# Masking attention by a VectorE multiply after exp in place of TensorE matmuls into the scores

## The chip, the cores and the metric

One core of one Trainium2 chip. The metric is the device time of one execution in microseconds (us). Medians of several executions are given; ratios are told apart from them below. An execution that took over 1.5% longer than the fastest of its kernel, at a lower granted clock, is marked slow and left out.

## The reference

Two layers, each run twice. Layer B (a gated MLP with a spatial matmul) isn't touched. Layer A is attention with a recurrent memory: 2048 tokens are cut into 64 segments of 32, and each segment attends over 8 memory rows and its own tokens. The first 8 output rows are the next segment's memory, so segments run one after the other.

```python
L = M + seg_len                                   # 8 + 32
mask = (idx[:, None] < M) | (idx[:, None] >= idx[None, :])
for s in range(n_seg):                            # 64, one after the other
    h = concatenate([mem, x_of_segment])
    q, k, v = h @ Wq, h @ Wk, h @ Wv              # 32 heads of 128
    scores = where(mask, q k^T * scale, -1e9)
    o = softmax(scores) v @ Wo
    mem = o[:, :M]                                # feeds the next segment
```

## The kernel before

32 heads are worked in two score tiles (r = 0 and 1). A score tile packs two heads side by side, so a mask is needed both for causality and for the blocks in which one head's queries meet the other's keys. The mask of 0 and -30000 is put into PSUM first, by an identity matmul for each half of the partitions; the score matmuls follow with start=False, to add to it.

```python
def scores(r):
    psS = att.tile([P, 4, 112], F32, name="psS")
    for g in range(2):                                           # the mask, by matmul
        nc.tensor.matmul(psS[64*g:64*g+64], lhsT=ident_bf[:, 64*g:64*g+64],
                         rhs=maskN[:, j4, :].unsqueeze(1).to_broadcast([P, 4, 112]),
                         start=True, stop=True, ...)
    for i in range(4):
        for K, hi, c0 in ((KA, 40, 0), (KTB, 16, 80)):
            for g in range(2):
                nc.tensor.matmul(psS[64*g:64*g+64, i, c0:c0+2*hi], lhsT=K[...], rhs=QQ[...],
                                 start=False, stop=True, ...)
    E[r] = segp.tile([P, 4, 112], BF16, name="E")
    nc.scalar.activation(out=E[r][:], in_=psS[:], func=ACT.Exp, scale=scale)

def denom(r):   # sums by matmul with ones, then 1/x as exp(-ln x), on ScalarE
    nc.tensor.matmul(psD[:], lhsT=ones64[:], rhs=E[r][:, :, 0:80], ...)
    ...
    nc.scalar.activation(out=L[:], in_=psD[:], func=ACT.Ln)
    nc.scalar.activation(out=R[r][:], in_=L[:], func=ACT.Exp, scale=-1.0)

# one segment; the order on TensorE, VectorE and ScalarE is the program's (cut)
r0 = qk(0); r2 = qk(2); qk_T(0, r0); r1 = qk(1); qk_T(2, r2); r3 = qk(3); qk_T(1, r1)
scores(0)
qk_T(3, r3)                  # VectorE transpose of the last K rows
v0 = v_mm(0, range(KT))
denom(0)
v_out(0, v0)
scores(1)
probs(0)
v1 = v_mm(1, range(KT)); v_out(1, v1)
denom(1)
...                          # pv(0), output projection, pv(1), next segment's input
```

The softmax here doesn't subtract the row's maximum and nothing guards it: scores larger than these inputs give would overflow.

## Time and profile before

| | before |
|---|---|
| median (4 runs) | 2167.15 us (2165.07 to 2173.1) |
| TensorE, VectorE, ScalarE busy | 86%, 50%, 49% |
| segments | 128, in two stretches of 64 |
| undisturbed length of a segment | 12.18 us |
| mean length of a segment | 12.68 us |

"Undisturbed" is, here and below, the tenth percentile of the 126 steps from one segment's first projection matmul to the next one's. The mean is longer because TensorE stops for about 1 us in about every second segment. In the lines of the profile PE is TensorE (PEld its weight loads), DVE VectorE, ACT ScalarE, POOL GpSimd, and L400 is line 400 of the kernel. Two lines of the waits on TensorE itself (engine, line, what it waited for: us in total, times, longest) show most of these stops and where TensorE waits for the transposed input `hA`:

```profile
PE pw L493 <- issue: 48.5, 45, 3.7
PE psm L400 <- DVE hA L536: 38.0, 114, 0.7
```

### The profile page before, as it was taken

Reading aid. Unit: us, or ns where it says so; the run is one execution under the profiler, and the core shown is the slowest. Engines: PE = TensorE matmul, PEld = TensorE weight load, DVE = VectorE, ACT = ScalarE, POOL = GpSimd, SP = SyncE. Lnnn points to the kernel's source line nnn. Section 1 sums busy time; section 2 is a strip of 40 time slices with the busy share of each in tenths; the row PEclk is TensorE's granted clock in tenths of the full one; section 3 lists DMA queues with packets and bytes.
Section 4 is the critical chain, followed back from the end, with each engine's and each line's share of the span. In section 5 each row is a group of like instructions: output and inputs, shape, how many; then the busy total and the mean of one; then the engine's idle time right before and its main releaser. Section 6 shows DMA issues by size and latency. Waiting matters only on the chain. (4 is left out here: it accounts for less than half of the span.)

```text
span 2160.9 us, 102768 instructions
## 1 busy us (share of the span) xinstructions
PE 1865.7 (86%) x47588; PEld 1090.1 (50%) x47616; DVE 1087.1 (50%) x2419; ACT 1054.1 (49%) x2340; POOL 179.7 (8%) x319
## 2 busy tenths in 40 slices
PE   0699999999999998582987999999999999995899
PEld 0355555555555555341763555555555555554476
DVE  1555555555555555340434555555555555553322
ACT  0465555555555555380004555555555555554600
POOL 2000000000000000001230000000000000000022
PEclk9999999999999999895998999999999999998999
DMA  9201111111111110328552011111111111104253
GB/s 379 84 21 35 36 42 37 37 37 35 45 35 35 36 30 24 104 84 255 157 159 63 23 42 36 38 35 37 43 36 36 35 35 35 32 27 156 49 137 88
DMA packets 178670, 145.22 MB, mean 67 GB/s; under 512 B 97472, under 2 KB 148288, under 8 KB 175168
## 3 DMA queue, kind: packets, MB, share of 16 engines
q1 hardware_dynamic: 152544, 83.76, 14.2%
q10 hardware_dynamic: 21728, 30.78, 4.1%
q0 software_dynamic: 3968, 24.12, 2.9%
q8 instruction: 372, 6.09, 1.1%
q14 instruction: 58, 0.48, 0.1%
HBM read 88.13 MB, written 33.70 MB: 56 GB/s over the span
## 5 line engine op out<-in xcount | busy, mean ns | idle before, releaser
L400 PEld LDWEIGHTS <-hA 128*32 128x32 bf16 x12288 | 302.7, 96 | 349.4 <-DVE hA L536 93.2
L560 ACT CAST rows<-psm 128x512 bf16<-128x512 f32 x512 | 299.7, 585 | 187.7 <-PE psm L400 187.7
L493 PE MATMUL pw<-Wo_sb,uT 128*32 128x128 bf16 x16640 | 289.7, 220 | 58.8 <-issue 48.5
L400 PE MATMUL psm<-Wq_sb,hA 128*32 128x512 bf16 x4096 | 272.4, 382 | 38.3 <-DVE hA L536 38.0
L493 PEld LDWEIGHTS <-uT 128*32 128x32 bf16 x16640 | 240.0, 97 | 106.3 <-issue 56.5
L400 PE MATMUL psm<-Wk_sb,hA 128*32 128x512 bf16 x4096 | 270.7, 380 | 0.0
L400 PE MATMUL psv<-Wv_sb,hA 128*32 128x512 bf16 x4096 | 268.0, 382 | 0.0
L219 PE MATMUL pg<-wspT,z2n 128*128 128x256 bf16 (+1 forms) x1536 | 177.1, 277 | 55.7 <-DMA wspT<-in_B_w_sp_dram 55.7
L564 DVE STREAM_TRANSPOSE QQ<-rows 128x512 bf16<-128x512 bf16 x256 | 181.2, 708 | 82.2 <-ACT rows L560 80.3
L564 DVE STREAM_TRANSPOSE KA<-rows 128x512 bf16<-128x512 bf16 x256 | 182.1, 711 | 36.2 <-ACT rows L560 36.0
L573 DVE CAST VA<-psv 128x512 bf16<-128x512 f32 x256 | 177.0, 691 | 43.5 <-PE psv L400 27.6
L535 DVE CAST_PREDICATED pre<-maskM,pw 128x128 bf16<-128x128 uint16 x126 | 36.6, 291 | 321.2 <-PE pw L493 321.2
L219 PEld LDWEIGHTS <-z2n 128*128 128x128 bf16 (+1 forms) x1536 | 151.3, 100 | 81.2 <-issue 63.1
L602 ACT ACTIVATE L<-psD 128x320 f32<-128x320 f32 x256 | 111.9, 437 | 153.1 <-PE psD L600 153.1
L400 PE MATMUL psb<-Wq_sb,hB 128*32 128x512 bf16 x1024 | 80.7, 393 | 92.2 <-DVE hB L449 72.4
L609 DVE TENSOR_TENSOR PT<-E,R 128x320 bf16<-128x320 bf16 x256 | 83.3, 325 | 144.0 <-ACT R L604 144.0
L529 POOL COPY QQ<-QTB 128x256 bf16<-128x256 bf16 x128 | 49.4, 402 | 1211.3 <-PE psO L621 839.7
L222 DVE TENSOR_TENSOR gb<-pg,bsp_bc 128x256 f32<-128x256 f32 x96 | 40.6, 423 | 208.1 <-PE pg L219 208.1
L625 ACT CAST uT<-psO 128x128 bf16<-128x128 f32 x256 | 67.8, 265 | 145.5 <-PE psO L621 145.5
L590 ACT ACTIVATE E<-psS 128x448 bf16<-128x448 f32 x256 | 136.8, 534 | 0.0
L540 ACT COPY o_sb<-pw 128x128 f32<-128x128 f32 x130 | 34.5, 265 | 194.2 <-DVE pre L535 181.6
L400 PEld LDWEIGHTS <-hB 128*32 128x32 bf16 x3072 | 57.1, 96 | 140.8 <-DVE hB L449 72.4
(93 smaller groups left out, 2613.6 us busy)
## 6 DMA issues: line engine op xcount, KB each, us to landing
xs<-xd SPq DMA_DIRECT2D x48, 256.0 KB
xs<-xd ACTq DMA_DIRECT2D x48, 256.0 KB
oA_d<-o_sb SPq DMA_DIRECT2D x130, 64.0 KB
xs_y<-xd SPq DMA_DIRECT2D x32, 256.0 KB
xd<-ot_y SPq DMA_DIRECT2D x32, 256.0 KB
Wq_sb<-in_A_Wq_dram POOLq DMA_DIRECT2D x6, 1024.0 KB, 16.1
Wk_sb<-in_A_Wk_dram POOLq DMA_DIRECT2D x6, 1024.0 KB, 24.5
Wv_sb<-in_A_Wv_dram POOLq DMA_DIRECT2D x6, 1024.0 KB, 20.5
```

The source lines that it names most:

```text
L219: nc.tensor.matmul(pg[0:fsz, :], lhsT=z2n[:, st_i, f0:f0 + fsz], rhs=wspT[:, st_i, :], start=(st_i == 0), stop=(st_i == NT - 1))
L222: nc.vector.tensor_tensor(out=gb[0:fsz, :], in0=pg[0:fsz, :], in1=bsp_bc[0:fsz, t0:t0 + TC2], op=ALU.add)
L400: nc.tensor.matmul(ps[32 * cg:32 * cg + 32, :], lhsT=lhs(kt, cg), rhs=rhs(kt, cg), start=(kt == 0), stop=(kt == KT - 1), tile_position=(0, ...
L493: nc.tensor.matmul(po[32 * cg:32 * cg + 32, 0:128], lhsT=lhs[:, n, :], rhs=wo_rhs(h, cg), start=(h == 0), stop=(h == H - 1), tile_position ...
L529: nc.gpsimd.tensor_copy(QQ[:, :, :, 0:8], bs["QTB"][:, :, :, 8 * j4:8 * j4 + 8])
L560: nc.scalar.copy(r[:], ps[:])
L564: nc.vector.transpose(out=QQ[:, j % 2, :, 8:40] if j < 2 else KA[:, j % 2], in_=r[:])
L573: nc.vector.tensor_copy(VA[:, r].rearrange("p i e -> p (i e)"), ps[:])
L590: nc.scalar.activation(out=E[r][:], in_=psS[:], func=ACT.Exp, scale=scale)
L602: nc.scalar.activation(out=L[:], in_=psD[:], func=ACT.Ln)
L609: nc.vector.tensor_tensor(out=PT[r][:, :, 0:80], in0=E[r][:, :, 0:80], in1=R[r][:], op=ALU.mult)
L625: nc.scalar.copy(hview(uT_cur, r, 0, 8), ov[:, :, :, 8:16])
```

## The change

The intent: TensorE is the busiest engine, VectorE is idle half of the time, so the mask moves to VectorE. The mask becomes 0 and 1, is multiplied into exp(scores), and the four mask matmuls of a segment go.

```diff
-    nc.gpsimd.memset(maskf[:], NEG)
+    nc.gpsimd.memset(maskf[:], 0.0)
     ... (allowed places 1.0 in place of 0.0, fill 0.0 in place of NEG)
 def scores(r):
-    for g in range(2):
-        nc.tensor.matmul(psS[64*g:64*g+64], lhsT=ident_bf[...], rhs=maskN[...], start=True, ...)
     ...
-                start=False, stop=True, ...)
+                start=(i == 0 and K is KA), stop=True, ...)
     ... exp as before ...
+def close(r):
+    nc.vector.tensor_tensor(out=E[r][:], in0=E[r][:],
+        in1=maskN[:, j4, :].unsqueeze(1).to_broadcast([P, 4, 112]), op=ALU.mult)
 ...
 scores(0)
 qk_T(3, r3)
+close(0)
 v0 = v_mm(0, range(KT))
 denom(0)
 v_out(0, v0)
 scores(1)
+close(1)
 probs(0)
```

More of the change, by code (lines that the diff above doesn't have):

```diff
@@ L25 @@
 FH = 688
-NEG = -30000.0
 LN_EXP_SET = 6
@@ L70, in _consts @@
             q = 32 * (2 * g + sl)
-            nc.gpsimd.memset(maskf[q:q + 32, :, 40 * sl:40 * sl + 40], 0.0)
-            nc.gpsimd.memset(maskf[q:q + 32, :, 80 + 16 * sl:96 + 16 * sl], 0.0)
+            nc.gpsimd.memset(maskf[q:q + 32, :, 40 * sl:40 * sl + 40], 1.0)
+            nc.gpsimd.memset(maskf[q:q + 32, :, 80 + 16 * sl:96 + 16 * sl], 1.0)
             blk = maskf[q:q + 32, :, 40 * sl + 16:40 * sl + 40]
-            nc.gpsimd.affine_select(out=blk, in_=blk, compare_op=ALU.is_ge, fill=NEG, base=8,
+            nc.gpsimd.affine_select(out=blk, in_=blk, compare_op=ALU.is_ge, fill=0.0, base=8,
                                     pattern=[[0, 4], [1, 24]], channel_multiplier=-1)
@@ L79, in _consts @@
                 blk = maskf[q:q + 32, :, 80 + 16 * sl + lo:88 + 16 * sl + lo]
-                nc.gpsimd.affine_select(out=blk, in_=blk, compare_op=ALU.is_ge, fill=NEG, base=0,
+                nc.gpsimd.affine_select(out=blk, in_=blk, compare_op=ALU.is_ge, fill=0.0, base=0,
                                         pattern=[[-8, 4], [0, 8]], channel_multiplier=1)
-                nc.gpsimd.affine_select(out=blk, in_=blk, compare_op=ALU.is_ge, fill=NEG, base=0 if step else 7,
+                nc.gpsimd.affine_select(out=blk, in_=blk, compare_op=ALU.is_ge, fill=0.0, base=0 if step else 7,
                                         pattern=[[8, 4], [step, 8]], channel_multiplier=-1)
@@ L577, in scores @@
                 psS = att.tile([P, 4, 112], F32, name="psS")
-                for g in range(2):
-                    nc.tensor.matmul(psS[64 * g:64 * g + 64], lhsT=ident_bf[:, 64 * g:64 * g + 64],
-                                     rhs=maskN[:, j4, :].unsqueeze(1).to_broadcast([P, 4, 112]),
-                                     start=True, stop=True, tile_position=(0, 64 * g), skip_group_check=True)
                 for i in range(4):
@@ L587, in scores @@
                                              lhsT=K[:, r, n:n + 2, :].rearrange("p h k -> p (h k)"), rhs=QQ[:, r, n:n + 2, 0:hi],
-                                             start=False, stop=True, tile_position=(0, 64 * g), skip_group_check=True)
+                                             start=(i == 0 and K is KA), stop=True, tile_position=(0, 64 * g), skip_group_check=True)
                 E[r] = segp.tile([P, 4, 112], BF16, name="E")
                 nc.scalar.activation(out=E[r][:], in_=psS[:], func=ACT.Exp, scale=scale)
+            def close(r):
+                nc.vector.tensor_tensor(out=E[r][:], in0=E[r][:], in1=maskN[:, j4, :].unsqueeze(1).to_broadcast([P, 4, 112]), op=ALU.mult)
             def last(t, n):
```

## The prediction

> **What bounds the kernel now.** I read the busy table and the 40 slices first, to find the stage that the change touches.
>
> ```profile
> PE 1865.7 (86%) x47588; PEld 1090.1 (50%) x47616; DVE 1087.1 (50%) x2419; ACT 1054.1 (49%) x2340; POOL 179.7 (8%) x319
> ...
> PE   0699999999999998582987999999999999995899
> ...
> DVE  1555555555555555340434555555555555553322
> ```
>
> TensorE looks nearly full and VectorE half empty, in two long even stretches (the two attention blocks). Each is 64 segments run one after the other: a segment's output becomes the next one's memory. In the trace the first projection matmuls of the segments start at 79.1 to 880.7 us in the first block and 1153.3 to 1949.8 us in the second: 12.72 and 12.64 us a segment (63 steps each). The undisturbed period is 12.18 us; the other half microsecond is mostly stops of about 1 us in the output-projection matmuls, put down to "issue". So 128 segments hold some 1620 of the 2166.8 us, and 0.1 us in one segment is 13 us in the kernel. The other two stages are untouched.
>
> Next the groups, shapes apart, for what is removed and for the yardstick of what is added.
>
> ```profile
> L579 PE MATMUL psS<-maskN,ident_bf 128*64 128x448 bf16 x512 | 97.4, 377 | 0.0
> ...
> L609 DVE TENSOR_TENSOR PT<-E,R 128x320 bf16<-128x320 bf16 x256 | 83.3, 325 | 144.0 <-ACT R L604 144.0
> ...
> L610 DVE TENSOR_TENSOR PT<-E,R 128x128 bf16<-128x128 bf16 x256 | 56.1, 219 | 0.0
> ```
>
> 512 mask matmuls, two for each of two score tiles in 128 segments. Their 97.4 us are not what they cost, since matmuls overlap. That, and everything else that decides this case, stands in the timeline of one segment (start us, duration us):
>
> ```profile
> 408.58 0.71 DVE L564 STREAM_TRANSPOSE KA<-rows 128x512 bf16<-128x512 bf16 x1
> ...
> 409.57 0.38 PE L579 MATMUL psS<-maskN,ident_bf 128*64 128x448 bf16 x2
> ...
> 409.69 0.58 ACT L560 CAST rows<-psm 128x512 bf16<-128x512 f32 x1 [0.28 <-PE psm L400]
> 409.79 0.20 PE L586 MATMUL psS<-QQ,KA 128*64 128x80 bf16 x2
> ...
> 410.14 1.05 PE L400 MATMUL psv<-Wv_sb,hA 128*32 128x512 bf16 x16
> 410.25 0.54 ACT L590 ACTIVATE E<-psS 128x448 bf16<-128x448 f32 x1
> 410.31 0.71 DVE L564 STREAM_TRANSPOSE KA<-rows 128x512 bf16<-128x512 bf16 x1 [0.15 <-ACT rows L560]
> ...
> 411.24 0.69 DVE L573 CAST VA<-psv 128x512 bf16<-128x512 f32 x1 [0.21 <-PE psv L400]
> ...
> 411.41 0.38 PE L579 MATMUL psS<-maskN,ident_bf 128*64 128x448 bf16 x2
> ...
> 411.98 1.05 PE L400 MATMUL psv<-Wv_sb,hA 128*32 128x512 bf16 x16
> 411.99 0.47 ACT L604 ACTIVATE R<-L 128x320 bf16<-128x320 f32 x1
> 412.36 0.53 ACT L590 ACTIVATE E<-psS 128x448 bf16<-128x448 f32 x1
> 412.49 0.32 DVE L609 TENSOR_TENSOR PT<-E,R 128x320 bf16<-128x320 bf16 x1 [0.56 <-ACT R L604]
> ...
> 412.95 0.31 PE L599 MATMUL psD<-E,ones 128*128 128x320 bf16 x1
> ...
> 413.80 0.21 PE L621 MATMUL psO<-PT,VA 64*128 64x80 bf16 x2
> ```
>
> Three things are to be seen. A mask pair delays the scores by 409.79 - 409.57 = 0.22 us. The first exp (410.25) begins when ScalarE has finished the last row copy (409.69 + 0.58 = 410.27), so it hangs on ScalarE, not on the mask. And the second exp ends at 412.89, the second denominator matmul starts at 412.95: exp and TensorE arrive together there, with no slack for anything put between them.
>
> [...] 325 ns for 320 elements and 219 for 128 give 0.55 ns per element[...]. [...]
>
> **The change part by part.** Removed: four matmuls and their weight loads a segment, 2 x 0.22 = 0.44 us of TensorE's order. The constants differ only in value. Moved: nothing else on TensorE or ScalarE; on VectorE the built order is last K transpose, multiply 0, V copy 0, multiply 1, probabilities 0, V copy 1. Added: 256 VectorE products of 448 elements, in place in E, two a segment. From L609: 325 + 128 x 0.55 = 396 ns, 0.40 us each. The denominator matmul waited for exp; it now waits for the product.
>
> I now run the shown segment forward with its own durations, with 0.05 us from VectorE's end to TensorE's start (hA ends 405.95, its matmul starts 406.00) and 0.03 us from ScalarE to VectorE (R ends 412.46, L609 starts 412.49).
>
> First half. Scores end 0.22 earlier, but exp 0 still starts at 410.25 behind the row copy and ends 410.79. VectorE is in the last K transpose until 411.02. Multiply 0 runs 411.02 to 411.42, so denominator 0 starts at 411.47, not 411.11: later by 0.36. TensorE has finished its V matmuls by then (they start 0.22 earlier) and waits over half a microsecond. The first saving is lost.
>
> Second half. Log, reciprocal-exp and exp 1 follow denominator 0 on ScalarE in fixed order: exp 1 moves from 412.36 to 412.72 and ends 413.25. The second saving shortens TensorE's road to the scores, which is not what exp 1 waits for, so it is lost too. Multiply 1: 413.28 to 413.68. Denominator 1: 413.73 in place of 412.95, later by 0.78.
>
> The rest. The first PV matmul stood 0.85 after denominator 1, behind other projection work: 414.58. It needs probabilities 0, now behind multiply 1: 413.68 plus 0.46 (412.49 to 412.95 today) = 414.14, in time. Probabilities 1, output projection, memory copy and next segment follow at the same distances.
>
> Sum: +0.36 (multiply 0 behind the transpose) + 0.42 (multiply 1 whole, with its extra hand-over) = 0.78 us. Back-to-back VectorE starts overlap by some 0.03, so I take 0.75: x 128 = 96 us. 2166.8 + 96 = 2263; I take nothing off for the issue stops, which the longer waits might hide a little.
>
> **The rivals.** (a) TensorE sets the pace and the matmuls' time is saved: 0.44 x 128 = 56 us, 2111 us. For it: 86% busy and back-to-back matmuls. Against it: ScalarE's row copy before exp 0 and the exp-to-denominator tie. It could only be if the multiply hid, and nothing in the order lies between it and its matmul. (b) One of the two multiplies hides, say if the first denominator is later but exp 1 isn't: about 0.4 x 128 = 50 us, 2215 us. The fixed ScalarE order speaks against it. (c) [...] 148 + 448 x 1.10 = 640 ns, 0.24 more per multiply, all on the path: 0.75 + 0.48 = 1.23 x 128 = 157 us, 2324 us. For it: the mask is a repeated row[...]. (d) The 1 us issue stops, 0.5 us a segment, fall differently because a segment has eight TensorE instructions fewer and pauses twice: between 25 us gained and 15 us lost, an estimate from 64 us of them in all.
>
> **Range and chances.** The order of the three engines is fixed, so I trust the sign more than the size. Centre 2263. Down to 2230 if issue stops shrink or some of the 0.36 hides; up to 2305 for slower multiplies in part or extra waits after multiply 1. Faster by over 2% (under 2123) needs (a): 0.03. Within 2% (up to 2210) needs (b) and (d) together: 0.07. Slower: 0.90.
>
> **What would show each step.** Right: the product lasts near 400 ns; it follows directly on the last K transpose; denominator 0 waits for it on TensorE (0.5 us or more), denominator 1 too; exp 0 starts no earlier after the segment's start (4.25 us); undisturbed segments take about 12.95 us; TensorE's share falls below 82%; the other two stages keep their time. Wrong: a product of 600 ns (rival c); no TensorE wait at the denominators; exp 0 earlier by 0.2 us, which would mean that the mask did delay it; or a period of 12.18 us or less.

The sum: 0.36 + 0.42 = 0.78 us, taken as 0.75 us, x 128 = 96 us, so 2263 us. The overlap of 0.03 us is found in the trace between two transposes of the shown segment (QQ, 407.93 + 0.68 = 408.61, and KA, which starts at 408.58; 28 ns in the median of 26 such pairs). Rival (c) supposes that reading the mask row again and again doubles the time of an element, 1.10 ns in place of the 0.55 from L609 and L610. That the moved start flag suffices was not shown either: kernels with it passed the comparison with the reference ("Another order on VectorE" and "exp 1 ahead of the reciprocal of tile 0"), though that comparison doesn't see the mask, as "No mask at all" will show. The score matmuls took 208 and 184 ns in the mean with it, 202 and 182 before.

## The result and the profile after

The changed kernel takes 2255.7 us (median of 4 runs, 2254.7 to 2261.1) against 2167.15. The ratio is 1.0409, 95% interval 1.0383 to 1.0435: slower. Ratios here and below are from fast runs alone; they are not quite the ratios of the medians.

The busy table and slices of the changed kernel:

```profile
PE 1834.6 (81%) x47076; PEld 1079.0 (48%) x47104; DVE 1142.5 (51%) x2675; ACT 1045.2 (46%) x2340; POOL 179.1 (8%) x319
...
PE   0688888888888888582977888888888888885899
...
DVE  2555555555555555340334555555555555553422
```

TensorE has 512 matmuls fewer (47588 to 47076), and its share falls from 86% to 81%: slices of nine tenths have become slices of eight. Less work there did not make a shorter kernel. The groups and the list of waits say where the room went:

```profile
L588 DVE TENSOR_TENSOR E<-E,maskN 128x448 bf16<-128x448 bf16 x256 | 99.1, 387 | 159.3 <-ACT E L585 159.3
L597 PE MATMUL psD<-E,ones 128*128 128x320 bf16 x256 | 75.9, 296 | 117.5 <-DVE E L588 117.5
```

```profile
DVE E L588 <- ACT E L585: 159.3, 128, 1.2
PE psD L597 <- DVE E L588: 117.5, 256, 1.4
```

The multiply takes 387 ns in the mean. All 256 denominator matmuls now wait for it, 117.5 us in total, 0.92 us a segment; before, TensorE had no such wait. VectorE in turn stands idle 159.3 us, 128 times, until exp 1 gives it its operand: its idle time lies before the operand is there, where the multiply can't use it. One segment of the changed kernel, starting at 439.39 us (start, duration):

```profile
443.08 0.58 ACT L559 CAST rows<-psm 128x512 bf16<-128x512 f32 x1 [0.28 <-PE psm L399]
...
443.56 0.55 ACT L585 ACTIVATE E<-psS 128x448 bf16<-128x448 f32 x1
443.70 0.71 DVE L563 STREAM_TRANSPOSE KA<-rows 128x512 bf16<-128x512 bf16 x1 [0.15 <-ACT rows L559]
444.33 0.35 DVE L588 TENSOR_TENSOR E<-E,maskN 128x448 bf16<-128x448 bf16 x1
...
444.74 0.30 PE L597 MATMUL psD<-E,ones 128*128 128x320 bf16 x1 [0.35 <-DVE E L588]
...
445.59 0.47 ACT L602 ACTIVATE R<-L 128x320 bf16<-128x320 f32 x1
445.97 0.53 ACT L585 ACTIVATE E<-psS 128x448 bf16<-128x448 f32 x1
446.53 0.39 DVE L588 TENSOR_TENSOR E<-E,maskN 128x448 bf16<-128x448 bf16 x1 [1.25 <-ACT E L585]
...
446.97 0.30 PE L597 MATMUL psD<-E,ones 128*128 128x320 bf16 x1 [0.53 <-DVE E L588]
```

Multiply 0 follows at once on the last K transpose, though exp 0 had ended 0.22 us earlier (443.56 + 0.55 = 444.11); the denominator follows at once on the multiply. Multiply 1 follows on exp 1, which follows on R, the reciprocal of tile 0, on ScalarE.

Starts within a segment, in us after its first projection matmul, from the two traces (medians over the 29 and 32 segments within 0.03 us of the undisturbed length):

| | before | after | difference |
|---|---|---|---|
| exp 0 | 4.24 | 4.17 | -0.07 |
| multiply 0 | | 4.94 | |
| denominator 0 | 5.11 | 5.35 | +0.24 |
| exp 1 | 6.36 | 6.58 | +0.22 |
| multiply 1 | | 7.14 | |
| denominator 1 | 6.95 | 7.58 | +0.63 |
| next segment | 12.18 | 12.80 | +0.62 |

After denominator 1 the two kernels run in step. The mean segment went from 12.68 to 13.43 us, more than the undisturbed one, because the stops rose from 0.50 to 0.63 us a segment. In the profiled runs, 98.3 us apart, the two stretches of 63 steps account for 1691.9 - 1598.0 = 93.9 us; the stretch between them grew by 6.0 us, the start by 0.4, and the end shrank by 2.1.

### The profile page after: what moved, and what is told of

It reads as the page before. It is cut to its first block, busy times and chain, and to the rows that moved or that the text cites. A ratio compares the mean times of both kernels' runs of the same rounds, so it can differ in the third digit from the quotient of the medians.

```text
span 2259.2 us, 102109 instructions
## 1 busy us (share of the span) xinstructions
PE 1834.6 (81%) x47076; PEld 1079.0 (48%) x47104; DVE 1142.5 (51%) x2675; ACT 1045.2 (46%) x2340; POOL 179.1 (8%) x319
## 5 line engine op out<-in xcount | busy, mean ns | idle before, releaser
L588 DVE TENSOR_TENSOR E<-E,maskN 128x448 bf16<-128x448 bf16 x256 | 99.1, 387 | 159.3 <-ACT E L585 159.3
L597 PE MATMUL psD<-E,ones 128*128 128x320 bf16 x256 | 75.9, 296 | 117.5 <-DVE E L588 117.5
```

Of the source, the lines that this page charges most:

```text
L588: nc.vector.tensor_tensor(out=E[r][:], in0=E[r][:], in1=maskN[:, j4, :].unsqueeze(1).to_broadcast([P, 4, 112]), op=ALU.mult)
```

## The experiments

Nine runs of eight kernels were made, on two chips. Where the text speaks of a period, it is the undisturbed segment of that run's profile.

### Both masks at once

The mask matmuls stay as they were; a second mask of 0 and 1 is made at the start, and the two multiplies are added.

```diff
 # on the kernel before
+maskB = maskf * (1/30000) + 1
 scores(0); qk_T(3, r3)
+close(0)        # E *= maskB
 ...
 scores(1)
+close(1)
```

> Both ways at once: the mask matmuls of the kernel before stay and the two multiplies are added. Theory A (the multiplies' waits set the pace, TensorE's mask time is off the path): the undisturbed segment stays at the 12.80 us of the changed kernel, so 2167 + 128 x 0.62 = 2246 us, 2240 to 2262 with the issue stops. Rival B (TensorE's time adds up; removing the mask matmuls saved 0.44 us a segment and the multiplies cost 1.06): 13.24 us, 2303 us. Side question: with 704 TensorE instructions a segment again, the issue stops (mean less shortest period) go back from 0.63 to about 0.50 us [...], and stay at 0.63 if they hang on the waits.

2257.78 us (2254.41 to 2260.07), ratio to before 1.0395 (1.0374 to 1.0415); period 12.80 us. Putting all four matmuls back into the changed kernel costs nothing: multiplies, denominators, exp 1 and the next segment start within 0.01 us of where they do in the changed kernel. The waits on TensorE show where they went:

```profile
PE psD L607 <- DVE E L598: 66.2, 256, 0.6
```

66.2 us of waiting in place of 117.5: 51.3 / 128 = 0.40 us a segment, near the 0.44 that four mask matmuls take. In the changed kernel nearly all of TensorE's saved time is turned into waiting. Rival B falls. The side question: the stops stayed at some 0.62 us a segment with the old number of instructions, so that number alone doesn't set them. Nor do the multiplies' waits alone: the kernels without a multiply, below, have 0.59 to 0.64.

### One multiply each

```diff
 # e2_first: close(0) and no mask matmuls for tile 0; tile 1 as before
 # e3_second: close(1) and no mask matmuls for tile 1; tile 0 as before
```

> Multiply for the first score tile alone, mask matmuls for the second. Theory A: only denominator 0 is late, behind the last K transpose, by 0.24 us: period 12.42 us, 2167 + 31 = 2198 us. Rival C (each multiply costs its own 0.4 us less a share of the saved matmuls, the same for both tiles): half of the loss, 2211 us for this and the next run alike.

> Multiply for the second score tile alone, mask matmuls for the first. Theory A: the whole multiply and its hand-over stand between exp 1 and denominator 1, where there was no slack: 0.42 us, period 12.60 us, 2167 + 54 = 2221 us; more than the first tile's. Rival C: 2211 us.

The first alone: 2206.42 us, ratio 1.0156 (1.0139 to 1.0174), period 12.40 us, denominator 0 at 5.35. The second alone: 2229.93 us, ratio 1.0271 (1.0246 to 1.0296), period 12.58 us, denominator 1 at 7.36 against 6.95. The same instruction costs 0.22 us in one place and 0.40 in the other; together 0.62, which is the whole change. Rival C, which has both cost the same, falls: the two intervals don't touch. Both medians lie 8 to 9 us above the expectation: the kernel before took 2172.08 us on this chip, 5 us above the 2167 that I reckoned from, and the stops were 0.64 us a segment in both in place of 0.50.

### No mask at all

```diff
 # e4_nomask: the mask matmuls removed, no multiply (a wrong result on purpose)
```

> No mask at all, neither matmuls nor multiplies: a wrong result on purpose, to see what a mask that costs nothing would be worth. Theory A: TensorE and the chain exp 0, denominator 0, log, reciprocal, exp 1, denominator 1 are tied, and the chain moves only by the first 0.22 us: period 11.96 us, 2167 - 28 = 2139 us. Rival B: both pairs count, 0.44 us, 11.74 us, 2111 us.

Period 11.96 us, as theory A has it; rival B's 11.74 falls. Four executions took 2141.08, 2147.69, 2174.37 and 2176.37 us. The last two, and with them the profiled one, are slow (granted clock 0.965 and 0.964, against 0.971 and 0.972 of the other two); the ratio of the fast two is 0.987 (0.984 to 0.9899). In the slow profile all stretches of half clock lie outside the 126 steps (the segments' Q projection matmuls took 382 ns in the mean, as in the kernel before), so its period may be read, and its total may not. A mask that cost nothing would be worth 0.22 us a segment and not 0.44.

The comparison with the reference at the outputs' tolerance doesn't see the mask, so for none of these kernels is it evidence that the mask is right. That the changed kernel masks the same places was checked by reading alone: the conditions of its selects are the old ones, with 1 and 0 for 0 and -30000.

### Another order on VectorE

```diff
 # on the changed kernel
 scores(0)
-qk_T(3, r3)
-close(0)
+close(0)
+qk_T(3, r3)
 ...
-close(1)
-probs(0)
+probs(0)
+close(1)
```

> The changed kernel with another order on VectorE: multiply 0 ahead of the last K transpose, probabilities 0 ahead of multiply 1. Theory A: multiply 0 starts right after exp 0 and denominator 0 comes at 5.16 us after the segment's start in place of 5.35, but the K transpose ends at 5.77 in place of 5.03 and the scores of tile 1 wait for it; exp 1 then hangs on ScalarE again: period 12.64 us, about 20 us less than the changed kernel, 2235 us. Rival D (the order doesn't matter, only the multiplies' length): 2256 us.

2236.68 us (2233.49 to 2240.49), period 12.66 us. Denominator 0 comes at 5.20, not 5.35, and exp 1 at 6.43, not 6.58: 0.14 us a segment better, near the expected 0.16, and still far behind the kernel before. The scores of tile 1 now wait for the transpose:

```profile
PE psS L581 <- DVE KA L563: 34.7, 128, 0.3
```

This wait isn't what holds exp 1: the scores end at 6.27, and exp 1 starts 0.09 us before the printed end of R, the same distance as in the changed kernel. The ratio to before, 1.0276, has a wide interval (1.0199 to 1.0352), as the kernel before ranged from 2164.7 to 2193.62 us on this chip; against the changed kernel's 2255.7 us the comparison is by period. Rival D falls by the period. Both moves were made in one run, so their shares aren't told apart by the period; the starts point to the first, since multiply 1 starts 0.03 us after exp 1's end in both kernels.

### Multiplies on GpSimd

```diff
-nc.vector.tensor_tensor(out=E[r][:], in0=E[r][:], in1=maskN...
+nc.gpsimd.tensor_tensor(out=E[r][:], in0=E[r][:], in1=maskN...
```

> The changed kernel with the multiplies on GpSimd, busy 8% of the time. GpSimd took 670 ns for 256 elements in the gated product of the other stage, so some 1.17 us for 448, an estimate. Theory A: both stand on the path whole: denominator 0 later by 0.92 us and denominator 1 by 2.15 against the kernel before, period 14.3 us, 2167 + 275 = 2442 us. Rival F (an idle engine hides the work): at or below the changed kernel's 2256 us.

2460.11 us (one run, its state unknown, granted clock 0.942), period 14.02 us. The groups:

```profile
L588 POOL TENSOR_TENSOR E<-E,maskN 128x448 bf16<-128x448 bf16 x256 | 263.9, 1031 | 1141.8 <-ACT E L585 1129.6 <-DVE KA L563 11.6 <-DMA preB<-xn_d 0.6
L597 PE MATMUL psD<-E,ones 128*128 128x320 bf16 x256 | 80.6, 315 | 283.8 <-POOL E L588 283.8
```

An engine that idled 92% of the time makes it worse: 1.03 us a product (my estimate was 1.17), 2.6 times the 0.39 us on VectorE. Denominator 0 comes 0.77 us later than in the kernel before, denominator 1 1.85. Rival F falls. What counts here is how long the operation lasts on its engine, not how idle the engine is. The total isn't a clean number: in this run alone TensorE's granted clock fell to half many times inside the attention blocks. The 36 of the 126 steps that met such a stretch took 16.28 us in the mean, the others 14.55. Why the clock fell isn't known.

### exp 1 ahead of the reciprocal of tile 0

The working holds ScalarE's fixed order responsible for carrying the lateness of denominator 0 to exp 1. Here the order is swapped.

```diff
 # on the changed kernel: denom() ends with Ln, recip() holds the Exp of -ln
 denom(0)
 v_out(0, v0)
 scores(1)          # exp 1
+recip(0)
 close(1)
 probs(0)
 ...
 denom(1)
+recip(1)
```

> The changed kernel with one swap on ScalarE: exp 1 ahead of the reciprocal-exp of tile 0. Theory A: the lateness of denominator 0 no longer reaches exp 1, which starts at some 6.17 us after the segment's start (when the log ends) in place of 6.58; multiply 1 from 6.73, denominator 1 at 7.17 in place of 7.58; probabilities 0 follow in time. Period 12.40 us, 2167 + 28 to 40 = 2195 to 2207 us. Rival G (multiply 1 itself, not ScalarE's order, holds denominator 1): 12.80 us, 2256 us.

2196.72 us (2191.3 to 2200.02), ratio 1.0093 (1.0029 to 1.0157), period 12.35 us. In one segment (starting at 426.12 us):

```profile
431.87 0.44 ACT L600 ACTIVATE L<-psD 128x320 f32<-128x320 f32 x1 [1.01 <-PE psD L598]
432.25 0.54 ACT L585 ACTIVATE E<-psS 128x448 bf16<-128x448 f32 x1
432.69 0.46 ACT L606 ACTIVATE R<-L 128x320 bf16<-128x320 f32 x1
432.82 0.39 DVE L588 TENSOR_TENSOR E<-E,maskN 128x448 bf16<-128x448 bf16 x1 [0.80 <-ACT E L585]
433.27 0.30 PE L597 MATMUL psD<-E,ones 128*128 128x320 bf16 x1
```

exp 1 begins as the log ends, and denominator 1 comes at 7.14 in place of 7.58. Swapping two instructions wins back 0.45 of the 0.62 us. Rival G falls. This is the best of the kernels that multiply both tiles, and still slower than before by some 0.9%.

### Mask matmuls in TensorE's hole

If the path is what counts, a mask matmul may stay on TensorE as long as it stands where TensorE waits anyway: at the segment's start.

```diff
 # on the kernel before; mask_mm() is the mask loop, taken out of scores()
+psS0 = mask_mm()
 r0 = qk(0)
 ...
-scores(0)
+scores(0, psS0)
 ...
-scores(1)
+scores(1, mask_mm())
```

> The kernel before, no multiply; the mask matmuls of tile 0 are issued at the segment's start, where TensorE waits 0.31 us for the transposed input. Theory A: 0.22 us leave the path before denominator 0 and the rest follows, as with no mask at all: period 11.96 us, 2139 us, with the right result. Rival E (ScalarE's row copy holds exp 0 and the chain behind it whatever TensorE does): 12.18 us, 2167 us.

> The same kernel as the run with the mask matmuls of tile 0 in TensorE's wait at the segment's start, again, in five rounds, since the first one's times spread from 2155 to 2181 us with the granted clock. Theory A: the period of 11.99 us against 12.18 is 0.19 x 128 = 24 us, so a ratio near 0.989 in runs of one clock. Rival: the gain is eaten elsewhere (the profile showed the stretch between the attention blocks longer by 29 us at a lower clock): ratio 0.995 to 1.00 again.

The period is 11.99 us in both runs, the same as with no mask at all within 0.03. The timeline shows the pair beside the transpose that TensorE used to wait for:

```profile
404.76 0.38 PE L578 MATMUL psS<-maskN,ident_bf 128*64 128x448 bf16 x2
404.77 0.31 DVE L536 STREAM_TRANSPOSE hA<-pre 128x128 bf16<-128x128 bf16 x1
405.14 1.05 PE L400 MATMUL psm<-Wq_sb,hA 128*32 128x512 bf16 x16
```

The wait for `hA`, 38.0 us in the kernel before, is 3.1 us here. The times are less clear. First run: 2164.93 us (2154.95 to 2180.67), ratio 0.9956 (0.9875 to 1.0036). Five rounds more: 2153.95 us (2151.21 to 2179.15), ratio 0.9933 (0.9859 to 1.0006), while the kernel before took 2164.7 to 2193.62 on that chip. Every interval includes 1, so a gain isn't established by the totals. They go with the granted clock: at 0.970 or more the six executions of this kernel took 2151.21 to 2156.68 us, the three of the kernel before on that chip 2164.7 to 2166.5. As these were picked out afterwards, they are a hint of some 12 us and no proof. Of 24 us that the period promises, the profile of the second run shows 13.2 in the two stretches (1584.8 against 1598.0 us for 126 steps); the stops took the rest, 0.59 us a segment against 0.50.

## Why the prediction was right

It gave 2263 us, the range 2230 to 2305 and 0.90 for slower; 2255.7 us came. By its steps:

- **The length of the multiply.** 0.40 us was worked out from L609; 0.39 was measured when it had waited and 0.35 when it followed directly on another VectorE instruction. Rival (c), 640 ns at twice the 0.55 ns an element, is out for a row of 112 read 4 times: the mean of all 256 products is 387 ns.
- **Exp 0 doesn't move.** Slightly wrong: it starts 0.07 us earlier (4.17, not 4.24). In the kernel before, the last score matmul ends at 4.20, so the mask did hold exp 0; without the mask exp 0 starts 0.10 us before the printed end of the row copy (4.27), which the prediction had read as the limit. It did no good, since multiply 0 still waited for the transpose.
- **First half, +0.36.** Right in mechanism, too large: 0.24 us. VectorE starts multiply 0 some 0.08 us before the printed end of the transpose (443.70 + 0.71 = 444.41, multiply 0 starts 444.33; the median of 128 such pairs is 0.076), and the multiply in such a row is the shorter one. I had taken 0.03 off for both hand-overs together. The kernel before shows the 0.08 already, in the pair that served as the yardstick (the median of all 256 pairs is 0.083):

```profile
425.88 0.33 DVE L609 TENSOR_TENSOR PT<-E,R 128x320 bf16<-128x320 bf16 x1 [0.56 <-ACT R L604]
426.12 0.22 DVE L610 TENSOR_TENSOR PT<-E,R 128x128 bf16<-128x128 bf16 x1
```

  So the prediction's 148 ns of fixed cost mixed L609, which had waited, with L610, which had not. Two that had waited, L609 and multiply 1, give (392 - 325) / 128 = 0.52 ns an element. L610 adds only 0.22 - 0.08 = 0.14 us for its 128 elements, of which 0.07 is then fixed. Multiply 0, with 0.35 - 0.08 = 0.27 us for 448 elements, has some 0.04 at this slope. Both fixed parts are estimates from these durations.
- **The wait of denominator 0.** Foretold as 0.5 us or more; 0.35 is printed, mostly for the same reason. That of denominator 1 is 0.53.
- **Second half, +0.42.** Right: 0.39 from the table (0.63 - 0.24), 0.40 when run alone. The ScalarE order as its carrier was shown by swapping it.
- **Both savings on TensorE lost.** Right, and shown by putting the matmuls back: no change in the period. Without any multiply the first of them does count: 0.22 us in the run without a mask, 0.19 in those with the pair moved to TensorE's hole.
- **Undisturbed segment 12.95.** 12.80 measured, for the first term above. 0.62 x 128 = 79 us.
- **Stops, nothing taken off.** They rose by 0.13 us a segment, 13.43 - 12.80 against 12.68 - 12.18, or 17 us. This made up, by luck, for the 0.13 us too much in the sum, so the total is closer than its parts. Rival (d) had listed at most 15 us of loss.
- **Rivals (a) and (b).** Out, by the runs with both masks and with one multiply each.

What stays open is why the stops differ. They were 0.50 us a segment in the profile of before and 0.59 to 0.64 in all other kernels but the GpSimd one, whether these had 704 TensorE instructions a segment or fewer. The GpSimd run's 1.03 goes with the half clock: in its segments at full clock it is 0.53. Only one profile of the kernel before was taken, so chance isn't excluded. In the changed kernel's segments 74 gaps of over 0.4 us between the starts of TensorE's matmuls and weight loads are put down to "issue", 1.03 us in the mean and 76 us in all; 60 of them lie in the output projection. Of the 73 distances between them 71 are 768, 1280 or 2048 such instructions, to within two. What makes these stops isn't shown.

## What to carry to other kernels

Before moving work from a busy engine to an idle one, look at whether the new place lies between two instructions that already follow on each other: here exp 1 and the denominator matmul, with 0.06 us between them. There an operation costs its whole length and its hand-overs, however idle its engine is: 0.40 us. Behind exp 0 there were 0.32 us to spare (4.79 to 5.11), and the same multiply, though it had to stand behind the transpose, cost 0.22. Work on the busy engine, in turn, can be almost free in the period if it stands in one of its waits: 11.99 us with tile 0's mask pair there, 11.96 us with no mask at all. In a chain across engines, the fixed order on an engine that the change doesn't touch may carry a delay on: here the 0.24 us of denominator 0 reached exp 1 as 0.22 us. Swapping two instructions there won back 0.45 of the 0.62 us.
